# A gated mix of linear attention and a Mish MLP on one core: features sent through DRAM, and the first block's numerator as one group

## The chip, the cores and the metric

The kernel runs on one core of a Trainium2 chip, in one launch. The metric is device time in microseconds (us), the median of three runs; lower is better.

## What is computed

The input x has 2048 rows (S) of 512 features (D). A gate per row mixes two branches. Cut to what matters:

```python
g = sigmoid((x * gate_w).sum(-1, keepdims=True))
q, k, v = x @ wqkv                        # H = 32 heads of Dh = 16
pq, pk = q @ w_phi[h], k @ w_phi[h]       # per head
phi(p) = concat(softmax(p), softmax(-p))  # over the 16 features of a head, 32 in all
kv  = phi(pk)^T v ;  z = sum over rows of phi(pk)
num = phi(pq) kv ;   den = phi(pq) z + 1e-6
a   = (num / den) @ wo
b   = mish(x @ w1 + b1) @ w2              # 512 -> 1376 -> 512
out = g * a + (1 - g) * b
```

## The kernel before

Every large product is made of three float32r products on TensorE: high part times high part, high times low, low times high. So each operand has a high copy (made by ScalarE) and a low remainder (made by VectorE or GpSimd).

A first half (eight chunks of 256 rows) projects k, v and q, takes the features of k, sums kv and z, and stores the projected q of each tile of 128 rows in DRAM (`pqd`). The second half, which the change touches, runs over four blocks of 512 rows (b = 0 to 3). A block has two kinds of work:

- **The MLP.** For each of eleven slices i of the hidden features: `up` (12 matmuls, w1 times x), `mi` (Mish, ScalarE), `hi` (high copy, ScalarE), `lo` (low remainder, GpSimd, line L503), and `dn` (12 matmuls, times w2, into four PSUM banks that stay open for the whole block). The last slice's `dn` is called `df0` to `df3`, one for each tile of 128 rows.
- **The attention of four tiles t of 128 rows.** `lq` loads the projected q from `pqd`. `mx mn d0 d1` (VectorE) subtract the maximum and the minimum, `E` (ScalarE) takes the exponential, `S rS` the sums and their reciprocals, `T D m de rd sc` the denominator, `es` scales the features by it, `tr` transposes them in 32 by 32 blocks in place. `mv` moves the features of two tiles (h = 0 or 1) into the layout `eT` that TensorE needs. `nu` (32 small matmuls for each h) makes the numerator in two PSUM banks, `oh` (ScalarE) and `ol` (VectorE, L611) copy it as high and low parts, `wo` (12 matmuls a tile) multiplies by the output weights, `ag` (ScalarE) scales by the gate, `fi` (VectorE, and a store) adds the MLP part.

`XH` and `XL` make the next block's x copies, after `LX` has loaded it; `ge gg` are the gate; `WH WL` split the output weights once, in block 0; `@z` makes the sums z.

The order is written out by hand, as a string of step names for each block (`BLOCK0`, `BLOCK1`, and `BLOCK` for blocks 2 and 3). `run` calls the steps in that order; a `+` means that the step belongs to the next block. `keep_in_program_order` pins every instruction, so each engine, and SyncE's DMA queue too, executes its own instructions in the order of the string, and an instruction that waits holds up all that stand behind it on its engine. What makes an instruction wait is its operands, and its buffers: a tile of a pool comes from a ring of a few slots by tag, and a step that takes a slot waits until all readers of the slot's last tile are done. Four rings matter here:

- PSUM: `a` (three banks: `up`, `nu`, `wo`), `kv` (one bank: `nu`, `wo`), `dn` (four).
- `oh`: two slots of 128x1024. A block's four `ohl` tiles (two for each h) take turns in them.
- `E`: two slots, each the features of a pair of tiles; `eT`: two slots.
- `pq`: three slots, for the loads `lq` and the gate row.

The move of the features before:

```python
for q in range(4):
    for k in range(4):
        o = 64 * (k % 2) + 32 * (k // 2)
        pin(Sy.dma_start(eTs[h][o : o + 32, :, q, :], Ep[key, h][32 * q : 32 * q + 32, :, k * 256 : (k + 1) * 256]))
```

Of the kernel before, what the change touches and what calls it, by code (L numbers as in the profile page):

```python
# [8 lines left out]
F32 = mybir.dt.float32  # L9
# [5 lines left out]
P = 128  # L15
S = 2048
D = 512
# [41 lines left out]


BLOCK0 = """
    up0 mi0 hi0 lo0 gr lq3 ldo0 ldo1 S1 rS1 mx2 mn2 d02 d12 up1 @z mi1 hi1 lo1 T0 D0 m0 de0 rd0 sc0 es0 tr0 up2 mi2 hi2 lo2 dn0
    T1 D1 m1 de1 rd1 sc1 es1 tr1 mv0 lq0+ lq1+ mx3 mn3 d03 d13 up3 mi3 hi3 lo3 WH0 dn1
    up4 mi4 hi4 lo4 WH1 WL0 dn2 E2 S2 T2 rS2 D2 m2 de2 rd2 sc2 es2 tr2 up5 mi5 hi5 lo5 WL1 dn3 E3 ge gg up6 mi6 hi6 lo6 dn4
    up7 mi7 hi7 lo7 dn5 nu0 oh0 S3 T3 rS3 ol0 D3 m3 de3 rd3 sc3 es3 tr3 mv1 up8 mi8 hi8 lo8 dn6
    mx0+ mn0+ d00+ d10+ mx1+ mn1+ d01+ d11+ lq2+ lq3+ wo0 ag0 wo1 ag1 E0+ E1+ S0+ T0+ rS0+ D0+ m0+ de0+ rd0+ sc0+ es0+ tr0+
    up9 mi9 hi9 lo9 dn7 up10 mi10 hi10 lo10 dn8 S1+ nu1 oh1 ol1 T1+ rS1+ D1+ LX0 LX1 m1+ de1+ rd1+ sc1+ es1+ tr1+ mv0+
    XH0+ XL0+ XH1+ XL1+ dn9 wo2 ag2 wo3 ag3 df0 fi0 df1 fi1 df2 fi2 df3 fi3
"""
BLOCK1 = """  # L70
    up0 mi0 hi0 lo0 gr mx2 mn2 d02 d12 mx3 mn3 d03 d13 up1 mi1 hi1 lo1 E2 E3 S2 T2 rS2 D2 m2 de2 rd2 sc2 es2 tr2
# [17 lines left out]
def tile_gated_mix(ctx: ExitStack, tc: tile.TileContext, xT, wv, wkT, wqT, bd, w1a, w1b, b1, w2a, w2b, wo, out):  # L89
# [6 lines left out]
    pin = tc.keep_in_program_order  # L96
    V, G_, A_, Sy = nc.vector, nc.gpsimd, nc.scalar, nc.sync

    def mm(*a, **k):
        return pin(nc.tensor.matmul(*a, **k))  # L100

    def T(shape, dt, tag, bufs, name):
        nm[0] += 1
        return sp.tile(shape, dt, name=f"{name}_{nm[0]}", tag=tag, bufs=bufs)

    def k8(name, tag, dt=F32R):
        return T([P, 2048], dt, tag, 2 if tag in ("eT", "E") else 1, name)

    def k4(name, tag, dt=F32):
        return T([P, 1024], dt, tag, {"tx": 2, "oh": 2, "z": 1}[tag], name)  # L110

    def k2(name, tag, dt=F32):
        return T([P, 512], dt, tag, {"pq": 3, "io": 4, "hl": 8}[tag], name)

    def psum(name, tag, bufs={"a": 3, "dn": 4, "kv": 1}):
        nm[0] += 1
        return pp.tile([P, 512], F32, name=f"{name}_{nm[0]}", tag=tag, bufs=bufs[tag])

    def act(out_, in_, fn=AF.Copy, **k):
        return pin(A_.activation(out_, in_, fn, **k))  # L120
# [4 lines left out]
    def hv(ap):  # L125
        return ap.rearrange("p (h f) -> p h f", f=DH)

    def f32(ap):
        return ap.bitcast(F32)
# [69 lines left out]
    def at(key, name, fn):  # L199
        steps.setdefault((key, name), []).append(fn)  # L200
# [10 lines left out]
    xs, Es, vs, psA, Ep = {}, {}, {}, {}, {}  # L211
# [38 lines left out]
    def feat_ops(key, t, src, d):  # L250

        n = str(t)

        def red(name, op):
            d[name] = T([P, H], F32, name, 2, name)
            pin(V.tensor_reduce(d[name], hv(src()), axis=AX.X, op=op))  # L256

        def dd(a):
            if "E" not in d:
                pair = key, t // 2  # L260
                if key == ("A", NCH - 1):
                    d["E"] = k4("E", "oh")
                else:
                    if pair not in Ep:
                        Ep[pair] = k8("E", "E", F32)[:, :].rearrange("p (t x) -> p t x", t=2)
                    d["E"] = Ep[pair][:, t % 2, :]
            E = hv(d["E"][:, a * 512 : (a + 1) * 512])
            if a == 0:
                pin(V.tensor_sub(E, hv(src()), d["mx"][:, :, None].to_broadcast([P, H, DH])))
            else:  # L270
                pin(V.tensor_sub(E, d["mn"][:, :, None].to_broadcast([P, H, DH]), hv(src())))  # L271

        def ss():
            d["S"] = T([P, 2 * H], F32, "Sm", 2, "Sm")
            pin(V.tensor_reduce(d["S"], hv(d["E"][:, :]), axis=AX.X, op=ALU.add))  # L275

        at(key, "mx" + n, lambda: red("mx", ALU.max))
        at(key, "mn" + n, lambda: red("mn", ALU.min))
        at(key, "d0" + n, lambda: dd(0))
        at(key, "d1" + n, lambda: dd(1))  # L280
        at(key, "E" + n, lambda: act(d["E"], d["E"], AF.Exp))
        at(key, "S" + n, ss)
        at(key, "rS" + n, lambda: pin(V.reciprocal(d["S"], d["S"])))

    def scale_by(d, eng):
        pin(eng.tensor_mul(hv(d["E"][:, :]), hv(d["E"][:, :]), d["S"][:, :, None].to_broadcast([P, 2 * H, DH])))  # L286
# [189 lines left out]

    def b_ops(b):
        key = ("B", b)
        U, dn, eTs, num, ohl, io = {}, {}, {}, {}, {}, {}

        def up(i):
            f = ORDER[i]
# [63 lines left out]
        for t in range(4):  # L546
            d = {}

            def lq(t=t, d=d):
                i = 4 * b + t  # L550
                d["p"] = k2("pq", "pq")
                pin(Sy.dma_start(d["p"], pqd[i * P : (i + 1) * P, :]))

            def tm(d=d):
                d["T"] = k4("T", "tx")
                pin(V.tensor_mul(d["T"], d["E"], B["zb"]))  # L556

            def dsum(d=d):
                d["D"] = T([P, 2 * H], F32, "Dn", 2, "Dn")
                pin(V.tensor_reduce(d["D"], hv(d["T"][:, :]), axis=AX.X, op=ALU.add))  # L560

            def de(d=d):
                d["d"] = T([P, H], F32, "den", 2, "den")
                pin(V.scalar_tensor_tensor(d["d"], d["D"][:, :H], 1e-6, d["D"][:, H:], op0=ALU.add, op1=ALU.add))  # L564

            def sc(d=d):
                sv = d["S"][:, :].rearrange("p (a h) -> p a h", a=2)
                pin(V.tensor_mul(sv, sv, d["d"][:, None, :].to_broadcast([P, 2, H])))

            def tr(d=d):  # L570
                pin(V.transpose(d["E"][:, :], d["E"][:, :]))

            at(key, f"lq{t}", lq)
            feat_ops(key, t, lambda d=d: d["p"][:, :], d)
            at(key, f"T{t}", tm)
            at(key, f"D{t}", dsum)
            at(key, f"m{t}", lambda d=d: pin(V.tensor_mul(d["D"], d["D"], d["S"])))
            at(key, f"de{t}", de)
            at(key, f"rd{t}", lambda d=d: pin(V.reciprocal(d["d"], d["d"])))
            at(key, f"sc{t}", sc)  # L580
            at(key, f"es{t}", lambda d=d: scale_by(d, V))
            at(key, f"tr{t}", tr)


        for h in range(2):
            def mv(h=h):
                eTs[h] = k8("eT", "eT", F32)[:, :].rearrange("p (t q x) -> p t q x", t=2, q=4)
                for q in range(4):
                    for k in range(4):
                        o = 64 * (k % 2) + 32 * (k // 2)  # L590
                        pin(Sy.dma_start(eTs[h][o : o + 32, :, q, :], Ep[key, h][32 * q : 32 * q + 32, :, k * 256 : (k + 1) * 256]))  # L591

            def nu(h=h):
                ev = eTs[h][:, :, :, :].rearrange("p t q (b c) -> p b (t q) c", c=32)
                po = [psum("num", tag) for tag in (("a", "a") if b and h else ("kv", "a"))]
                for bh in range(2):
                    for c in range(4):
                        u = 4 * bh + c
                        for r in range(2):
                            mm(po[r][32 * c : 32 * c + 32, bh * SC : (bh + 1) * SC], kvb[64 * r : 64 * r + 64, u, :], ev[64 * r : 64 * r + 64, u, :, :], start=True, stop=True, skip_group_check=True)  # L600
                for r in range(2):
                    num[h, r] = po[r]

            def oh(h=h):
                for gp in range(2):
                    ohl[h, gp] = k4("ohl", "oh", F32R)
                    act(ohl[h, gp][:, :512], num[h, gp])

            def ol(h=h):
                for gp in range(2):  # L610
                    pin(V.tensor_sub(ohl[h, gp][:, 512:], num[h, gp], f32(ohl[h, gp][:, :512])))  # L611

            at(key, f"mv{h}", mv)
            at(key, f"nu{h}", nu)
            at(key, f"oh{h}", oh)
            at(key, f"ol{h}", ol)
# [59 lines left out]
    for b in range(NB):  # L676
        b_ops(b)
# [47 lines left out]
    for j in range(2):  # L725
        h, l = [w[:, 2 * j : 2 * j + 2, :].rearrange("p k f -> p (k f)") for w in (wvh, wvl)]
# [94 lines left out]
```

## Time and profile before

| | |
|---|---|
| median of 3 runs | 451.55 us (450.78 to 451.81) |
| the profiled execution | 449.86 us, of which the span is 448.1 us |
| TensorE (PE) busy | 442.7 us, 99% of the span |
| VectorE (DVE) busy | 312.6 us, 70% |
| ScalarE (ACT) busy | 194.0 us, 43% |
| GpSimd (POOL) busy | 162.2 us, 36% |
| mean granted TensorE clock | 0.999 |
| DMA traffic | 40.20 MB in 27177 packets, mean 90 GB/s |

A busy share says how long an engine had an instruction in hand; matmuls are pipelined, so a busy TensorE can still have small holes. Times in the traces are microseconds from the start of the span. PEld is TensorE's weight load, SPq is SyncE's DMA queue. In a group of rows, "x12" is the number of instructions; in brackets stand the idle time before and who ended it.

### The profile page before, as it was taken

To read this page: it belongs to the slowest core of one execution; us is meant where nothing else is said; L and a number is where in the kernel's file an instruction comes from. 1 tells how busy PE (TensorE), PEld (TensorE's weight loads), DVE (VectorE), ACT (ScalarE), POOL (GpSimd) and SP (SyncE) were. 2 spreads that over 40 slices of the span, in tenths; PEclk is the share of its full clock that TensorE was granted. 3 is DMA by queue.
4 is the path that set the end of the run, shared out by engine and by line. 5 is a ranking of instruction groups with operands and counts; after the bars stand their busy time and mean duration, and the time that the engine had idled before them with its cause. 6 is when DMAs were issued, how large, how long until landed. Compare 5 with 4: busy or idle time off the path is not lost.

```text
span 448.1 us, 7219 instructions
## 1 busy us (share of the span) xinstructions
PE 442.7 (99%) x2878; PEld 363.5 (81%) x2878; DVE 312.6 (70%) x412; ACT 194.0 (43%) x267; POOL 162.2 (36%) x101
## 2 busy tenths in 40 slices
PE   8999999999999999999999999999999999999997
PEld 7888888888888888778788878888878888887885
DVE  3797658559399999999989998369769329701103
ACT  3644433444325457527165352644262653242330
POOL 3448686677862253511132220214220222221121
PEclk9999999999999999999999999999999999999999
DMA  7721522514511122313433141321231302030002
GB/s 270 272 95 47 191 80 84 191 32 155 190 49 47 48 65 66 93 49 90 147 99 136 40 151 53 88 95 47 66 123 48 94 2 94 17 78 1 0 1 94
DMA packets 27177, 40.20 MB, mean 90 GB/s; under 512 B 6916, under 2 KB 15620, under 8 KB 27144
## 3 DMA queue, kind: packets, MB, share of 16 engines
q1 hardware_dynamic: 26824, 39.35, 28.0%
q8 instruction: 22, 0.36, 0.3%
q10 hardware_dynamic: 288, 0.39, 0.3%
q14 instruction: 11, 0.09, 0.1%
q0 software_dynamic: 32, 0.01, 0.0%
HBM read 22.82 MB, written 8.40 MB: 70 GB/s over the span
## 4 chain that ended last, share of the span: by engine, by line
PE 87%; DVE 9%; SPq 2%; issue 1%; DMA 0%; ACT 0%; DVEq 0%
PE proj L100 27%; PE down L100 23%; PE up L100 22%; PE wo L100 10%; PE num L100 2%; SPq L591 2%; PE kvp L100 1%; PE warm L100 1%; DVE xbl L409 1%; DVE Sm L275 1%; PE fuse L100 1%; DVE E L286 1%; DVE T L556 1%; DVE E L271 1%; DVE den L564 1%
## 5 line engine op out<-in xcount | busy, mean ns | idle before, releaser
L503 POOL TENSOR_TENSOR l<-act,h 128x512 fp32r<-128x512 f32 x44 | 62.6, 1425 | 222.1 <-ACT h L120 203.1
L120 ACT ACTIVATE act<-up,b1s 128x512 f32<-128x512 f32 x44 | 30.2, 687 | 87.6 <-PE up L100 86.7
L324 POOL TENSOR_TENSOR zacc<-zacc,E 128x1024 f32<-128x1024 f32 x16 | 39.7, 2482 | 42.7 <-DVE E L286 41.4
L120 ACT ACTIVATE E<-E 128x1024 f32<-128x1024 f32 x32 | 33.5, 1059 | 41.0 <-DVE E L271 40.9
L286 DVE TENSOR_TENSOR E<-E,Sm 128x1024 f32<-128x1024 f32 x32 | 45.6, 1426 | 1.1
L100 PE MATMUL wo<-woh,ohl 128*128 128x512 f32 x128 | 41.2, 389 | 0.0
L275 DVE TENSOR_REDUCE Sm<-E 128x64 f32<-128x1024 f32 x32 | 38.5, 1204 | 1.5 <-ACT E L120 1.5
L100 PE MATMUL down<-w2ah,h 128*128 128x512 f32 x96 | 37.6, 392 | 0.0
L100 PE MATMUL down<-w2al,h 128*128 128x512 f32 x96 | 37.4, 390 | 0.0
L100 PE MATMUL down<-w2ah,l 128*128 128x512 f32 x96 | 37.4, 389 | 0.0
L256 DVE TENSOR_REDUCE mx<-proj 128x32 f32<-128x512 f32 x16 | 11.0, 689 | 30.7 <-PE proj L100 30.7
L100 PE MATMUL down<-w2bh,h 128*128 128x512 f32 x78 | 30.6, 392 | 0.0
L409 DVE TENSOR_TENSOR xbl<-xraw,xbh 128x1024 fp32r<-128x1024 f32 x8 | 12.0, 1528 | 26.5 <-ACT xbh L120 26.5
L100 PE MATMUL down<-w2bl,h 128*128 128x512 f32 x78 | 30.4, 390 | 0.0
L100 PE MATMUL down<-w2bh,l 128*128 128x512 f32 x78 | 30.3, 389 | 0.0
L120 ACT ACTIVATE h<-act 128x512 fp32r<-128x512 f32 x44 | 27.8, 632 | 1.4
L100 PEld LDWEIGHTS wo<-woh,ohl 128*128 128x128 f32 x128 | 24.0, 188 | 5.0
L120 ACT ACTIVATE io<-wo,g_sb 128x512 f32<-128x512 f32 x16 | 10.9, 689 | 35.3 <-PE wo L100 35.3
L120 ACT ACT_TABLE_LOAD x19 | 24.4, 1283 | 3.8 <-PE up L100 3.5
L100 PE MATMUL up<-xbh,w1ah 128*128 128x512 f32 x96 | 25.8, 390 | 0.0
L100 PE MATMUL up<-xbl,w1ah 128*128 128x512 f32 x96 | 25.7, 389 | 0.0
L100 PE MATMUL up<-xbh,w1al 128*128 128x512 f32 x96 | 25.7, 389 | 0.0
(120 smaller groups left out, 971.5 us busy)
## 6 DMA issues: line engine op xcount, KB each, us to landing
eT<-E SPq DMA_DIRECT2D x128, 64.0 KB, 2.0
xraw<-in_xT_dram SPq DMA_DIRECT2D x15, 512.0 KB, 4.6
pqd<-qs SPq DMA_DIRECT2D x16, 256.0 KB, 3.1
pq<-pqd SPq DMA_DIRECT2D x16, 256.0 KB, 2.9
out_dram<-io SPq DMA_DIRECT2D x15, 256.0 KB, 2.1
raw<-in_w1a_dram SPq DMA_DIRECT2D x3, 512.0 KB, 4.4
raw<-in_w2a_dram SPq DMA_DIRECT2D x3, 512.0 KB, 4.2
wT<-in_wkT_dram SPq DMA_DIRECT2D x4, 256.0 KB, 4.5
```

The lines of the kernel that those rows point to most:

```text
L100: return pin(nc.tensor.matmul(*a, **k))
L120: return pin(A_.activation(out_, in_, fn, **k))
L256: pin(V.tensor_reduce(d[name], hv(src()), axis=AX.X, op=op))
L271: pin(V.tensor_sub(E, d["mn"][:, :, None].to_broadcast([P, H, DH]), hv(src())))
L275: pin(V.tensor_reduce(d["S"], hv(d["E"][:, :]), axis=AX.X, op=ALU.add))
L286: pin(eng.tensor_mul(hv(d["E"][:, :]), hv(d["E"][:, :]), d["S"][:, :, None].to_broadcast([P, 2 * H, DH])))
L324: at(key, f"z{t}", lambda d=d: pin(G_.tensor_add(zacc, zacc, d["E"])))
L409: pin(V.tensor_sub(xb[b][1][:, :, sl], kt(raw[h], SC), f32(xb[b][0][:, :, sl])))
L503: pin(G_.tensor_sub(U[i]["l"], U[i]["a"], f32(U[i]["h"])))
L556: pin(V.tensor_mul(d["T"], d["E"], B["zb"]))
L564: pin(V.scalar_tensor_tensor(d["d"], d["D"][:, :H], 1e-6, d["D"][:, H:], op0=ALU.add, op1=ALU.add))
L591: pin(Sy.dma_start(eTs[h][o : o + 32, :, q, :], Ep[key, h][32 * q : 32 * q + 32, :, k * 256 : (k + 1) * 256]))
```

## The change

Two things change.

The features go through DRAM. After `tr`, each tile's features (128x1024) are stored in a DRAM tile `ed`; `mv` then reads each tile's `ed` back with four loads (32 partitions x 4 x 256 elements each) in place of sixteen moves within SBUF for a pair. So a pair has two stores of 512 KB and eight loads of 128 KB, in all four blocks, and the store stands in SyncE's queue at the place of `tr`.

The order of block 0 changes. `nu0` and `nu1` stand together behind `dn9`, the tenth of the block's MLP tiles, and `df0` to `df3` follow them; all of `wo0` to `wo3` stand at the end of the block, with `fi` between them. `d02 d12` move behind the second tile's `tr`. In PSUM, the block's `nu` takes `kv` and `a` for h = 0 and `a` and `a` for h = 1, as the other blocks do already.

```diff
 BLOCK0 = """
-    up0 mi0 hi0 lo0 gr lq3 ldo0 ldo1 S1 rS1 mx2 mn2 d02 d12 up1 @z mi1 hi1 lo1 T0 D0 m0 de0 rd0 sc0 es0 tr0 up2 mi2 hi2 lo2 dn0
-    T1 D1 m1 de1 rd1 sc1 es1 tr1 mv0 lq0+ lq1+ mx3 mn3 d03 d13 up3 mi3 hi3 lo3 WH0 dn1
+    up0 mi0 hi0 lo0 gr lq3 ldo0 ldo1 S1 rS1 mx2 mn2 up1 @z mi1 hi1 lo1 T0 D0 m0 de0 rd0 sc0 es0 tr0 up2 mi2 hi2 lo2 dn0
+    T1 D1 m1 de1 rd1 sc1 es1 tr1 mv0 lq0+ lq1+ d02 d12 mx3 mn3 d03 d13 up3 mi3 hi3 lo3 WH0 dn1
     up4 mi4 hi4 lo4 WH1 WL0 dn2 E2 S2 T2 rS2 D2 m2 de2 rd2 sc2 es2 tr2 up5 mi5 hi5 lo5 WL1 dn3 E3 ge gg up6 mi6 hi6 lo6 dn4
-    up7 mi7 hi7 lo7 dn5 nu0 oh0 S3 T3 rS3 ol0 D3 m3 de3 rd3 sc3 es3 tr3 mv1 up8 mi8 hi8 lo8 dn6
-    mx0+ mn0+ d00+ d10+ mx1+ mn1+ d01+ d11+ lq2+ lq3+ wo0 ag0 wo1 ag1 E0+ E1+ S0+ T0+ rS0+ D0+ m0+ de0+ rd0+ sc0+ es0+ tr0+
-    up9 mi9 hi9 lo9 dn7 up10 mi10 hi10 lo10 dn8 S1+ nu1 oh1 ol1 T1+ rS1+ D1+ LX0 LX1 m1+ de1+ rd1+ sc1+ es1+ tr1+ mv0+
-    XH0+ XL0+ XH1+ XL1+ dn9 wo2 ag2 wo3 ag3 df0 fi0 df1 fi1 df2 fi2 df3 fi3
+    up7 mi7 hi7 lo7 dn5 S3 T3 rS3 D3 m3 de3 rd3 sc3 es3 tr3 mv1 up8 mi8 hi8 lo8 dn6
+    mx0+ mn0+ d00+ d10+ mx1+ mn1+ d01+ d11+ lq2+ lq3+ E0+ E1+ S0+ T0+ rS0+ D0+ m0+ de0+ rd0+ sc0+ es0+ tr0+
+    up9 mi9 hi9 lo9 dn7 up10 mi10 hi10 lo10 dn8 dn9 S1+ nu0 nu1 oh0 ol0 T1+ df0 df1 oh1 rS1+ D1+ LX0 LX1 ol1 df2 df3
+    wo0 ag0 m1+ de1+ rd1+ sc1+ es1+ fi0 XH0+ XL0+ wo1 ag1 fi1 wo2 ag2 XH1+ XL1+ fi2 tr1+ mv0+ wo3 ag3 fi3
 """
...
-            def tr(d=d):
+            def tr(t=t, d=d):
                 pin(V.transpose(d["E"][:, :], d["E"][:, :]))
+                ed[t] = tc.dram_tile([P, 2 * D], F32, name=f"ed{4 * b + t}")
+                pin(Sy.dma_start(ed[t], d["E"]))
...
                 eTs[h] = k8("eT", "eT", F32)[:, :].rearrange("p (t q x) -> p t q x", t=2, q=4)
-                for q in range(4):
+                for t in range(2):
+                    src = ed[2 * h + t].rearrange("(q p) x -> p q x", q=4)
                     for k in range(4):
                         o = 64 * (k % 2) + 32 * (k // 2)
-                        pin(Sy.dma_start(eTs[h][o : o + 32, :, q, :], Ep[key, h][32 * q : 32 * q + 32, :, k * 256 : (k + 1) * 256]))
+                        pin(Sy.dma_start(eTs[h][o : o + 32, t, :, :], src[:, :, k * 256 : (k + 1) * 256]))
...
-                po = [psum("num", tag) for tag in (("a", "a") if b and h else ("kv", "a"))]
+                po = [psum("num", tag) for tag in (("kv", "a"), ("a", "a"))[h]]
```

The strings of the other blocks are unchanged; in block 1 the steps around the third and fourth tile read `S3 T3 rS3 D3 m3 de3 rd3 sc3 es3 tr3 lq0+ lq1+ mv1 up3 ... mx0+ mn0+ d00+ d10+`.

More of the change, by code (lines that the diff above doesn't have):

```diff
@@ L478, in b_ops @@
         key = ("B", b)
-        U, dn, eTs, num, ohl, io = {}, {}, {}, {}, {}, {}
+        U, dn, eTs, num, ohl, io, ed = {}, {}, {}, {}, {}, {}, {}
         def up(i):
```

## The prediction

> **What bounds the kernel now.** I read the profile's page first, then what TensorE waited for, then the chain of waits.
>
> ```profile
> PE 442.7 (99%) x2878; PEld 363.5 (81%) x2878; DVE 312.6 (70%) x412; ACT 194.0 (43%) x267; POOL 162.2 (36%) x101
> PE 87%; DVE 9%; SPq 2%; issue 1%; DMA 0%; ACT 0%; DVEq 0%
> PE num L100 <- DMA eT<-E: 0.8, 1, 0.8
> ```
>
> TensorE is busy for 99% and in the whole of the second half waits once: at block 0's first `nu`, for the moved features. The chain shows what that costs:
>
> ```profile
> 190.44 1.60 PE num L100 x32
> 192.04 2.94 PE up L100 x12
> 214.02 1.02 PE num L100 x32
> 215.05 2.94 PE down L100 x12
> 226.15 8.16 PE up L100 x36
> 261.51 2.72 PE down L100 x12
> 264.23 1.89 PE num L100 x64
> 266.12 2.99 PE down L100 x12
> 269.10 5.44 PE wo L100 x24
> ```
>
> Twelve matmuls take 2.72 us everywhere, so TensorE's own work can't be shortened by an order; an order only removes or makes holes. Block 0's first `nu`: 0.83 waited, 1.60, and 0.22 more in the tile behind it (2.94 for 2.72), 2.65 in all. The second: 1.02 + 0.22, with rounding 1.25. Block 1 has both as one group: 1.89 + 0.27 = 2.16. The change makes block 0 like block 1, so it can gain 2.65 + 1.25 - 2.16 = **1.74 us**, and nothing else in the chain is there to gain.
>
> **What it adds: three new holes in TensorE's work.** In each an in-order engine, off the path until now, gets to set it.
>
> *First, `dn9` waits for `h9` (block 0).* Today `wo0 wo1 wo2 wo3` and the two `nu` stand among the last MLP tiles and give ScalarE time. Moved to the end, they uncover this:
>
> ```profile
> 189.22 0.39 PE L100 MATMUL down<-w2ah,l 128*128 128x512 f32 x1
> 205.97 0.69 DVE L271 TENSOR_TENSOR E<-mn,pq 128x512 f32<-128x512 f32 x1
> 206.69 1.06 ACT L120 ACTIVATE E<-E 128x1024 f32<-128x1024 f32 x1 [0.45 <-DVE E L271]
> 209.79 0.63 ACT L120 ACTIVATE h<-act 128x512 fp32r<-128x512 f32 x1
> 210.55 1.31 POOL L503 TENSOR_TENSOR l<-act,h 128x512 fp32r<-128x512 f32 x1 [12.69 <-ACT h L120]
> ```
>
> `dn5` issues its last matmul at 189.22, so the next tile can start at 189.45 (pitch 0.23, 2.72 over 12). Now `up8 dn6 up9 dn7 up10 dn8` follow without a gap, six tiles of 2.72, and `dn9` wants to start at 205.77. Its `h9` stands on ScalarE behind `E1+`, which waits for VectorE's `d11+`. From the end of `d11+` (206.66) to the end of `h9` (210.42) it is 3.76, to the end of `l9` on POOL (211.86) 5.2. So I need the new end of `d11+`. VectorE is never idle on the way there:
>
> ```profile
> 159.90 0.68 DVE L269 TENSOR_TENSOR E<-pq,mx 128x512 f32<-128x512 f32 x1
> 173.81 2.29 DVE L564 SCALAR_TENSOR_TENSOR den<-Dn 128x32 f32<-128x32 f32 x1
> 180.35 2.70 DVE L269 TENSOR_TENSOR E<-pq,mx 128x512 f32<-128x512 f32 x1
> 192.71 0.13 DVE L537 TENSOR_SCALAR ge_sb<-ge_sb 128x4 f32<-128x4 f32 x1
> 193.16 1.21 DVE L275 TENSOR_REDUCE Sm<-E 128x64 f32<-128x1024 f32 x1
> 195.42 0.54 DVE L283 RECIPROCAL Sm<-Sm 128x64 f32<-128x64 f32 x1
> 195.88 1.22 DVE L611 TENSOR_TENSOR ohl<-num,ohl 128x512 fp32r<-128x512 f32 x2
> 201.83 0.65 DVE L256 TENSOR_REDUCE mx<-pq 128x32 f32<-128x512 f32 x1
> 180.12 2.39 POOL L433 TENSOR_TENSOR wol<-raw,woh 128x1024 fp32r<-128x1024 f32 x1
> ```
>
> A tile of features (`S` to `tr`) takes 201.83 - 193.16 - 1.2 (the `ol` pair in it) = 7.5, without `S` (1.1) and `rS` (195.42 to 195.88) 5.9; eight operations `mx0+` to `d11+` take 206.66 - 201.83 = 4.8. From 159.90 on the new order has two tiles of 5.9, `d02 d12` 1.2 (two of the eight), `mx3` to `d13` 2.4, two tiles of 7.5, the gate 0.4 (192.71 to 193.16) and the 4.8: 35.6 us. Today's stretch has the `ol` pair too, 36.8, and takes 46.8: 10.0 are lost, as the rows at 173.81 and 180.35 show (the latter took 2.70 where the first row took 0.68, and ended with POOL's 2.39). An operation with two SBUF operands waits for POOL's subtraction, and the other way round; sums and transposes don't. POOL's ten subtractions stay, but meet other operations. Walking the new order with that rule I lose 1.3 at `de0`, 0.8 at `T1`, 2.3 at `d12` and 1.9 at `m2` (behind the two `wol`), 0.8 at `sc2`, 0.4 at `m3` and 0.3 in small ones, an estimate of 7.8: `d11+` ends at 159.9 + 35.6 + 7.8 = 203.3. Then `h9` is there at 207.1 (a wait of 1.3), and the third matmul, due 0.45 later, waits about 0.9 more for `l9` at 208.5: **2.2 us**. With 6 to 10 us lost, 0.5 to 4.5.
>
> *Second, `wo2` waits for `oh1` (block 0).* The tag `oh` has two slots and a block four `ohl` tiles. `oh1` now stands ahead of `wo0` on ScalarE, and can write only when `wo1`, the slots' last reader, is done with them; `ag0`, `XH0+` and all else on ScalarE queue behind it. `wo2` needs the bank `kv`, which `ag0` empties. So behind `wo1`'s last matmul stand in series the second half of `oh1` and `ag0`:
>
> ```profile
> 215.14 1.09 ACT L120 ACTIVATE ohl<-num 128x512 fp32r<-128x512 f32 x2 [2.38 <-PE num L100]
> 200.46 0.69 ACT L120 ACTIVATE io<-wo,g_sb 128x512 f32<-128x512 f32 x1 [4.03 <-PE wo L100]
> ```
>
> 0.55 + 0.69 and two hand-overs of about 0.1: **1.45 us** (1.25 to 2.0). The x copies of block 1 are no third wait here: `XH1+` follows `ag2`, and `wo3` (2.72) covers both.
>
> *Third, block 1's `mx0+` waits for its loads.* SyncE's queue holds `lq0+ lq1+` behind `tr3`. Until now `tr` issued no DMA, so the two loads left early; now the store of `tr3` stands ahead of them and waits for VectorE.
>
> ```profile
> 238.73 0.94 SPq L552 DMA_DIRECT2D pq<-pqd  x2
> 252.44 10.18 SPq L591 DMA_DIRECT2D eT<-E  x16
> 252.30 0.65 DVE L256 TENSOR_REDUCE mx<-pq 128x32 f32<-128x512 f32 x1
> 266.92 1.25 DVE L611 TENSOR_TENSOR ohl<-num,ohl 128x512 fp32r<-128x512 f32 x2
> DMA to landing us min/median/max: 2.6/2.9/5.7
> xraw<-in_xT_dram SPq DMA_DIRECT2D x15, 512.0 KB, 4.6
> ```
>
> The loads leave at 238.73 (0.47 each), and `mx0+` starts at 252.30 right behind `tr3`. In the changed kernel (times relative to the block's start) the store leaves at 252.44 and the first load 0.5 later. The line of landing times is for `pq`: 255.5 by its shortest, 258.6 by its longest. I take 256.4, its median 2.9 and 0.6 for the store's 512 KB ahead of it on the same queue, so VectorE is 4.1 us late (3.2 to 6.3). `E1+`, the gate and `tr0+` move with it, and so does `ol0`, whose first half empties the bank that `wo0` needs: 267.55 today, 1.55 ahead of `wo0` at 269.10. TensorE loses 4.1 - 1.5 = **2.6 us**; from both ends, with up to 0.6 regained where a meeting with POOL falls away, 1.1 to 4.8. Part of it shows earlier, as `nu1` waits for `mi7`.
>
> Block 2 has the same order, but a cover:
>
> ```profile
> 321.40 0.68 DVE L271 TENSOR_TENSOR E<-mn,pq 128x512 f32<-128x512 f32 x1
> 326.26 2.01 ACT L120 ACTIVATE E<-E 128x1024 f32<-128x1024 f32 x2
> ```
>
> There `d11+` ends at 322.08, and ScalarE comes to `E1+` only at 327.3: 5.2 us to spare against 4.1. Block 3 loads nothing. Both cost nothing; at the far end of 6.3 block 2 would cost 1.1.
>
> **What I cost at nothing.** `d02 d12` behind `tr1`: `E2` then waits for `d12` until 177.4 in my walk, and `h5` follows 3.76 later by the same chain as above, 181.2; `dn5` starts at 189.45 - 2.72 = 186.7, 5.5 to spare. `LX0 LX1` behind the store of `tr0+` in SyncE's queue: `LX1` waits for `D1+` anyway, about 217.5, lands 4.6 later at 222.1, and `XH1+` comes behind `wo2`, about 225.7. The other banks for `nu`: its last `a` bank waits for `mi10`, one ScalarE step (0.7) behind `h9`, at 207.8; `nu1` comes at 211.6 (below).
>
> **The route through DRAM itself**: nothing, as long as it lands in time.
>
> ```profile
> 179.31 10.20 SPq L591 DMA_DIRECT2D eT<-E  x16
> eT<-E SPq DMA_DIRECT2D x128, 64.0 KB, 2.0
> raw<-in_wo_dram SPq DMA_DIRECT2D x8, 128.0 KB, 3.1
> ```
>
> Today a pair lands 10.2 + 2.0 behind its `tr`. Now: the store 4.6, four loads at 10.2 / 16 = 0.64 each 2.6, landing 3.1: 10.3 (the other four go out while the store lands). In block 0 `tr3` ends at 203.3 - 4.8 = 198.5, so it lands at 208.8, and `nu1` comes at 205.77 + 2.2 + 2.72 + 0.95 = 211.6. The Trainium skill ("DMA: Bandwidth & Descriptors", "Anatomy of one DMA") puts a DMA at 2.0 us plus its bytes over 436 GB/s, measured on another issue path, and says that completion takes longest where HBM is written: by it the store is 3.2 and the sum the same. No run here shows a 512 KB store yet.
>
> **The sum.** -1.74 + 2.2 + 1.45 + 2.6 = +4.5 us. Against the profiled execution: 449.86 + 4.5 = 454.4. That execution lies 1.69 under the median of the runs; on the median, 451.55 + 4.5 = **456.0 us**. All low ends give +1.1, all high ends +9.6.
>
> **The rivals.**
> - *Not slower: VectorE escapes POOL.* If the new order meets none of POOL's subtractions in block 0, `d11+` ends at 195.5 and `dn9` doesn't wait; if block 1's `tr3` comes 2 us early likewise, the late loads cost 0.6 at most. Then -1.74 + 1.45 + 0 to 0.6: 451.3 to 451.9, no change. It decides where under 2 us are lost in block 0. For it: the losses are chance meetings. Against: ten subtractions remain and VectorE is full. Chance 0.06; a gain over 0.2% needs `oh1`'s wait gone too, which the slots forbid.
> - *Block 1's late loads are covered.* If they land sooner or the chain behind them has more room than the rows show, 2.6 drops out: 453.4. Chance 0.12.
> - *The DRAM trip is late.* If the store takes over 7.4 us (2.8 us to spare above), `nu1` waits, and in block 0 again as long as that excess, some 2 us: 458. Against: nothing else of weight is on the queue then. Chance 0.05.
> - *The clock falls.*
>
> ```profile
> 186.00:196.00 10.00, 9.17 (x66) 6.60 (x66) 9.72 (x15) 4.65 (x9) 2.53 (x2) 1.00 0.36 99
> ```
>
> In this window, with the hole of 0.83 in it, the clock granted is 1.00. At the high end of the first term `dn9` waits 3.5 in one piece, four times as long as any hole here. If the tile behind it then ran at half the clock, it would take 5.44 for 2.72: with the hole, 456.0 + 2.3 + 2.7 = 461. The Trainium skill ("TensorE: Matmul & The Clock Gate", "Part 1") has the clock halved after an idle window of about 3.4 us. No run here shows it. Chance 0.04.
>
> **How the numbers follow.** The forecast has 0.70; 0.03 is for what I haven't seen. About 0.2% (0.9 us) is what a measurement of this kernel can tell from no change. Range: down to 453.0 (block 1 covered, or two low ends), up to 459.0 (the high ends of two terms, or the late trip); outside lie "not slower", the clock, and the corners of the terms. Of the 0.06 I count 0.05 as same and 0.01 as faster, the unseen 0.03 as faster, and 0.01 of the covered case as same: faster 0.04, same 0.06, slower 0.90.
>
> **What would show it.** One `num` group of 64 in block 0, with no wait for a DMA. TensorE's waits: `down` for ACT `h` and POOL `l` (about 2), `wo` for ACT `io` (about 1.4), and in block 1 `num` and `wo` for ACT and DVE (about 2.6); VectorE waiting for `pq` in blocks 1 and 2, some 4 us each. In block 0 `d11+` ends near 203. I am wrong if `dn9` starts without a wait, or if `pq` lands ahead of `tr3`.

## The result, and the profile after

The changed kernel takes **457.69 us** (median of 5 runs, 456.93 to 459.22); the kernel before, run beside it, takes 450.93 (5 runs). The ratio is 1.0153, 95% interval 1.0130 to 1.0175: 6.8 us slower, where 4.5 were forecast on the median, and inside the range. Its profiled execution took 459.22 us with a span of 457.5, 9.4 more than the span before.

What TensorE waited for, after (total, times, longest, in us):

```profile
PE wo L100 <- DVE ohl L614: 2.1, 1, 2.1
PE down L100 <- ACT h L120: 1.3, 1, 1.3
PE wo L100 <- ACT io L120: 1.3, 1, 1.3
...
PE fuse L100 <- DMA wT<-in_wkT_dram: 0.9, 1, 0.9
PE down L100 <- POOL l L503: 0.7, 1, 0.7
```

The wait for the moved features is gone, and three holes have come: `dn9` for `h9` and `l9`, `wo2` for `ag0`, and block 1's `wo0` for `ol0`. The wait of `fuse` lies at the start, far ahead of the change, and differs from execution to execution: `dn5` ends 0.73 us later than before for that reason alone (first row below against 189.22).

The timeline of the three places, after (start, duration, engine, line, what; idle time in brackets). Line numbers behind the new store are two or three higher than before:

```profile
189.95 0.39 PE L100 MATMUL down<-w2ah,l 128*128 128x512 f32 x1
203.49 0.69 DVE L271 TENSOR_TENSOR E<-mn,pq 128x512 f32<-128x512 f32 x1
206.27 0.39 PE L100 MATMUL down<-w2bh,l 128*128 128x512 f32 x1
207.30 0.63 ACT L120 ACTIVATE h<-act 128x512 fp32r<-128x512 f32 x1
207.98 0.50 PE L100 MATMUL down<-w2bh,h 128*128 128x512 f32 x1 [1.32 <-ACT h L120]
208.06 2.54 POOL L503 TENSOR_TENSOR l<-act,h 128x512 fp32r<-128x512 f32 x2 [12.13 <-ACT h L120]
209.42 0.68 PE L100 MATMUL down<-w2bh,l 128*128 128x512 f32 x1 [0.71 <-POOL l L503]
209.90 0.63 PE L100 MATMUL down<-w2bh,h 128*128 128x512 f32 x1
212.46 0.63 PE L100 MATMUL down<-w2bh,h 128*128 128x512 f32 x1
213.49 1.96 PE L100 MATMUL num<-eT,kvb 64*32 64x256 f32 x64
223.87 0.60 ACT L120 ACTIVATE ohl<-num 128x512 fp32r<-128x512 f32 x1 [0.76 <-PE wo L100]
224.37 0.68 ACT L120 ACTIVATE io<-wo,g_sb 128x512 f32<-128x512 f32 x1
225.10 0.50 PE L100 MATMUL wo<-woh,ohl 128*128 128x512 f32 x1 [1.26 <-ACT io L120]
230.72 1.07 PE L100 MATMUL up<-xbh,w1ah 128*128 128x512 f32 x4
257.77 1.19 SPq L552 DMA_DIRECT2D pq<-pqd  x2
261.05 0.69 DVE L256 TENSOR_REDUCE mx<-pq 128x32 f32<-128x512 f32 x1 [3.68 <-DMA pq<-pqd]
268.89 2.60 PE L100 MATMUL num<-eT,kvb 64*32 64x256 f32 x64
276.54 0.50 PE L100 MATMUL wo<-woh,ohl 128*128 128x512 f32 x1 [2.07 <-DVE ohl L614]
```

Between 209.90 and 212.46 six matmuls go by: a pitch of 0.43 us where the forecast's is 0.23. The chain shows the same, and once more in block 1:

```profile
209.42 4.14 PE down L100 x10
...
218.40 5.45 PE wo L100 x24
276.54 7.35 PE wo L100 x24
```

The same 24 `wo` matmuls take 5.45 us in block 0 and 7.35 in block 1. The clock says why. The windows below lie on the grid that the clock's own changes give: each slow stretch is 3.41 us long, and from the end of the first to the start of the second it is 64.86 us, 19 times 3.41. Columns: length, PE busy (instructions), granted clock, DMA share, GB/s:

```profile
206.17:209.58 3.41, 1.38 (x6) 1.00 0.42 146
209.58:212.99 3.41, 3.41 (x9) 0.50 0.03 5
...
223.23:226.65 3.42, 2.15 (x10) 1.00 0.01 2
...
274.43:277.85 3.42, 1.35 (x7) 1.00 0.35 134
277.85:281.26 3.41, 3.41 (x10) 0.50 0.53 173
```

The window that holds both waits of `dn9` is idle for 2.03 of its 3.41 us, the one with block 1's hole for 2.07, and the window after each runs at half the clock. The one with `wo2`'s hole is idle for 1.26 and no slow one follows. A slow window costs 3.41 / 2 = 1.7 us, 0.0037 of the mean clock. The granted clocks of the five runs were 0.993, 0.993, 0.996, 0.996 and 1.000: two, two, one, one and no such windows. The median run is the one with none: its span of 454.8 us is the shortest of the five, but 2.9 us of its time lie outside the span, against 1.7 to 2.0 in the others. So the median comes out where the mean does (457.96 against 451.18 before, also 6.8 more) in part by chance.

The 9.4 us of the profiled pair then come out: 0.73 at the start; block 0 from `dn5` to block 1's first `up` 4.73 - 0.73 = 4.0 (230.72 above against the row of before below); in block 1 up to `wo0` 276.54 - 269.10 - 4.73 = 2.7; and 7.35 - 5.44 = 1.9 in the slow `wo`, of which some 0.2 is there at full clock too, as behind `wo2`'s hole. The row of before:

```profile
225.99 1.07 PE L100 MATMUL up<-xbh,w1ah 128*128 128x512 f32 x4
```

### The profile page after: what moved, and what is told of

Same layout as the page of the kernel before. It is cut to its first block, busy times and chain, and to the rows that moved or that the text cites. A ratio compares the mean times of both kernels' runs of the same rounds, so it can differ in the third digit from the quotient of the medians.

```text
span 457.5 us, 7152 instructions
## 1 busy us (share of the span) xinstructions
PE 446.4 (98%) x2878; PEld 365.1 (80%) x2878; DVE 312.6 (68%) x412; ACT 194.0 (42%) x267; POOL 160.6 (35%) x101
## 4 chain that ended last, share of the span: by engine, by line
PE 69%; DVE 23%; DMA 4%; issue 2%; ACT 1%; SPq 0%; POOL 0%; DVEq 0%; POOLq 0%
PE proj L100 25%; PE down L100 17%; PE up L100 15%; PE wo L100 9%; DVE E L286 2%; DVE Sm L275 2%; DVE T L556 2%; DVE E L571 2%; DMA wT<-in_wqT_dram 2%; DVE E L269 2%; DVE Dn L560 2%; DVE E L271 2%; DVE xbl L409 1%; DVE Dn L579 1%; DVE mn L256 1%
## 5 line engine op out<-in xcount | busy, mean ns | idle before, releaser
L503 POOL TENSOR_TENSOR l<-act,h 128x512 fp32r<-128x512 f32 x44 | 61.1, 1390 | 232.2 <-ACT h L120 210.7
L100 PE MATMUL wo<-woh,ohl 128*128 128x512 f32 x128 | 42.7, 402 | 3.3 <-DVE ohl L614 2.1
```

What stands on the lines that cost most here:

```text
L503: pin(G_.tensor_sub(U[i]["l"], U[i]["a"], f32(U[i]["h"])))
```

## The experiments

Three readings were set against each other: the **holes alone**, at the forecast's prices; **holes and clock**, where a hole can be followed by slow matmuls; and **the route**, that DRAM traffic itself costs the time. All medians:

| kernel | us | before beside it | ratio (95%) | granted clock of its runs |
|---|---|---|---|---|
| changed kernel | 457.69 | 450.93 | 1.0153 (1.0130 to 1.0175) | two at 0.993, two at 0.996, 1.000 |
| order alone | 453.92 | 451.19 | 1.0065 (1.0049 to 1.0081) | one of six at 0.995, the others 0.999 or 1.000 |
| route alone | 454.91 | 451.19 | 1.0085 (1.0059 to 1.0111) | three of six at 0.996 |
| route, early loads | 450.45 | 451.19 | 0.9984 (0.9971 to 0.9998) | all 0.999 or 1.000 |
| changed, `E0+ E1+` later | 456.39 | 451.19 | 1.0117 (1.0097 to 1.0137) | five of six at 0.996 |
| changed, `oh1` covered | 455.39 | 450.74 | 1.0095 (1.0077 to 1.0113) | 0.992, three at 0.996, two at 1.000 |
| changed, early loads | 453.24 | 450.59 | 1.0056 (1.0034 to 1.0079) | one of five at 0.996 |
| no holes | 449.24 | 450.74 | 0.9962 (0.9949 to 0.9975) | all 0.999 or 1.000 |
| no holes, old moves | 450.37 | 450.59 | 0.9992 (0.9976 to 1.0008) | all 0.999 or 1.000 |

**The order alone.** The changed kernel with the old `tr` and `mv`:

```diff
-ed[t] = tc.dram_tile(...); pin(Sy.dma_start(ed[t], d["E"]))
-pin(Sy.dma_start(eTs[h][o : o + 32, t, :, :], src[:, :, k * 256 : (k + 1) * 256]))
+pin(Sy.dma_start(eTs[h][o : o + 32, :, q, :], Ep[key, h][32 * q : 32 * q + 32, :, k * 256 : (k + 1) * 256]))
```

> The new order of block 0 and the new banks, with the old moves between SBUF tiles in place of the store and the loads. Holes alone (the forecast's terms): -1.7 for the merged num, +2.2 for dn9's wait, +1.4 for wo2's wait, nothing in block 1: 1.9 us over the kernel before. Holes and clock: the same, and where dn9's two waits fall into one stretch of some 3.4 us the following matmuls run at a pitch of 0.43 us, 1.6 to 2.1 more: 3.5 to 4.0 us over before in such a run. The route costs by itself (rival): the order alone then gives no more than 1 us over before.

Measured: 2.7 us over before (2.2 to 3.7 by the interval), more than the 1.9 of the holes alone. Its trace has the two waits of `dn9` to the hundredth, but on another phase of the grid:

```profile
208.38 0.50 PE L100 MATMUL down<-w2bh,h 128*128 128x512 f32 x1 [1.32 <-ACT h L120]
209.82 0.50 PE L100 MATMUL down<-w2bh,l 128*128 128x512 f32 x1 [0.71 <-POOL l L503]
```

```profile
205.92:209.33 3.41, 1.87 (x8) 1.00 0.38 97
209.33:212.74 3.41, 2.92 (x26) 1.00 0.62 168
```

A window's edge cuts the pair into 1.54 and 0.49 us of idle time, and the clock stays at 1.00. The same holes, with and without the slow tile: the clock's part is chance of phase, not of the kernel. The chain then shows what `dn9`'s holes cost at full clock. The ten matmuls behind the second wait:

```profile
209.82 2.60 PE down L100 x10
```

They take 2.60 where the changed kernel's took 4.14, so the slow window there cost 1.5. `dn9` was due at 206.90 (0.23 behind the last matmul of `dn8`, at 206.67) and starts at 208.38, 1.5 late; its third matmul, due 0.45 later, starts at 209.82, another 1.0 late; and some 0.2 go behind the holes. That is 2.7, not the forecast's 2.2: the waits that the profile lists (1.32 and 0.71) count only from the modelled end of the matmul before. With it the order alone costs -1.7 + 2.7 + 1.4 = 2.4, and one slow window in six runs 0.3: the measured 2.7.

**The route alone**, with the old order of block 0 and the old banks, and **the route with early loads**:

```diff
 BLOCK1: ... mx3 mn3 d03 d13
+lq0+ lq1+
 up1 ... es3 tr3
-lq0+ lq1+
 mv1 ...
 BLOCK (blocks 2, 3): up0 mi0 hi0 lo0 gr
+lq0+ lq1+
 S2 T2 ... es3 tr3
-lq0+ lq1+
 mv1 ...
```

> The store and the loads through DRAM, with the old order of block 0 and the old banks. Holes alone: block 1's mx0+ late by 3.7, TensorE loses 2.7 there; block 0's first num no longer waits for its moves (0.8 less at most): 1.9 to 2.7 us over before. Holes and clock: 1.9 more in a run where the 2.1 us before wo0 are followed by slow matmuls: 3.8 to 4.6. The route costs by itself: over 5 us.

> The route alone again, with lq0+ and lq1+ of blocks 1 and 2 put ahead of the stores in SyncE's queue. Holes alone, and holes and clock: no hole is left in block 1, the granted clock is 1.00 behind it, and the time is that of before, or up to 0.8 us less (block 0's first num without its wait). The route costs by itself: stays 2 us or more over before.

Measured: 3.7 us over before (2.7 to 5.0), and 0.7 under it (0.1 to 1.3). Moving two load instructions in a queue takes away all that the route costs, so the traffic itself costs nothing; what costs is the store that stands ahead of the loads. Nor did the first `num`'s 0.83 all come back. What TensorE waits for in the second kernel:

```profile
PE wo L100 <- DVE ohl L614: 0.9, 2, 0.6
```

These are two waits of block 0, of 0.30 and 0.55, that the kernel before doesn't have: where the features come earlier, VectorE's `ol0` and `ol1` are late.

**`dn9`'s hole taken out**:

```diff
-lq2+ lq3+ E0+ E1+ S0+ T0+ rS0+ D0+ m0+ de0+ rd0+ sc0+ es0+ tr0+ up9 mi9 hi9 lo9 dn7 up10
+lq2+ lq3+ up9 mi9 hi9 lo9 dn7 E0+ E1+ S0+ T0+ rS0+ D0+ m0+ de0+ rd0+ sc0+ es0+ tr0+ up10
```

> The changed kernel with E0+ E1+ and the steps behind them moved behind mi9 hi9 lo9, so that h9 no longer waits for VectorE's d11+. Holes alone: dn9 doesn't wait, 2.2 us under the changed kernel, 455.5. Holes and clock: 2.2 and the slow tile of 2.1 go, up to 4.3 us under the changed kernel in its slowest runs: 453.4 to 455.5, with a pitch of 0.23 us in dn9. If the clock fell for another reason than the hole, dn9 still runs at 0.43.

`dn9` doesn't wait and isn't slow, but the kernel gains only 1.3 us on the changed one's median. A new wait took the rest:

```profile
215.07 0.50 PE L100 MATMUL wo<-woh,ohl 128*128 128x512 f32 x1 [0.86 <-DVE ohl L614]
```

TensorE now comes earlier to `wo0`, and VectorE isn't ready with `ol0`, which stands behind `tr0+` and `S1+`. Of `dn9`'s 2.7 the wait and the restart behind it take back 1.1, which leaves 1.6; the clock would add up to 0.6 to that (five slow windows in six runs, against six in five). The medians show less than either, 1.3, and the expected 453.4 to 455.5 was missed; the runs don't show why beyond this wait.

**`wo2`'s hole taken out**: `oh1` and `ol1` behind `ag0` and close behind `wo1`, and half of `dn10` as cover.

```diff
-df0 df1 oh1 rS1+ D1+ LX0 LX1 ol1 df2 df3 wo0 ag0 m1+ de1+ rd1+ sc1+ es1+ fi0 XH0+ XL0+ wo1 ag1 fi1 wo2
+df0 df1 rS1+ D1+ LX0 LX1 wo0 ag0 m1+ de1+ rd1+ sc1+ wo1 oh1 ol1 es1+ ag1 XH0+ XL0+ XH1+ XL1+ df2 df3 fi0 fi1 wo2
```

> The changed kernel with oh1 and ol1 behind ag0 on ScalarE and with df2 df3 between wo1 and wo2 as cover. Holes alone: wo2's wait of 1.4 goes, dn9's and block 1's stay: 1.4 under the changed kernel, 456.2, in a run of equal granted clock. Holes and clock: the same; the clock's share of some 2 us for each slow window still comes and goes with dn9's and block 1's holes. If wo2's wait has another cause than the oh slots, it stays at 1.3.

The wait for `io` is gone, the other two stand unchanged (1.3 and 0.7; 2.1). The median is 2.3 us under the changed kernel: 1.4 for the hole, and some 0.6 for the clock, again with five slow windows in six runs. So it was `oh1`'s place ahead of `ag0`, where it waits for its slots, that cost the time.

**Block 1's hole taken out**: the changed kernel with the early loads above.

> The changed kernel with lq0+ and lq1+ of blocks 1 and 2 ahead of the stores, and nothing else. Holes alone: block 1's 2.7 us go, dn9's and wo2's stay: 455.0 from the changed kernel's 457.7. Holes and clock: with them goes the slow window behind that hole, which came in some two of three runs and costs 1.7: 453.9, that is 2.7 to 3.2 over before; the granted clock falls only where dn9's two waits lie in one window of the grid. The route costs by itself: 455 or more with no wait in block 1.

2.65 us over before, 4.45 under the changed kernel: the 2.7 of the hole, and 1.7 for one slow window a run less (one in five runs, against six). In its profiled run `dn9`'s two waits lie in one window of the grid again, with less idle time than any other that was followed by a slow one:

```profile
205.95:209.36 3.41, 1.49 (x5) 1.00 0.29 106
209.37:212.78 3.41, 3.41 (x16) 0.50 0.02 5
```

**No holes**: all three edits, with `ol0` ahead of `tr0+ S1+` and `T1+ D1+` drawn forward, so that VectorE is in time:

```diff
-es0+ tr0+ up10 mi10 hi10 lo10 dn8 dn9 S1+ nu0 nu1 oh0 ol0 T1+ df0 df1 oh1 rS1+ D1+ LX0 LX1 ol1 df2 df3 wo0 ...
+es0+ up10 mi10 hi10 lo10 dn8 dn9 nu0 nu1 oh0 ol0 T1+ D1+ LX0 LX1 tr0+ S1+ rS1+ df0 df1 wo0 ag0
+m1+ de1+ rd1+ sc1+ wo1 oh1 ol1 es1+ ag1 XH0+ XL0+ XH1+ XL1+ df2 df3 fi0 fi1 wo2 ag2 fi2 tr1+ mv0+ wo3 ag3 fi3
```

> All three holes taken out of the changed kernel: E0+ E1+ behind hi9, the features of the next block spread around the merged num so that ol0 and ol1 come in time, oh1 behind ag0 with df2 df3 as cover, lq0+ lq1+ of blocks 1 and 2 ahead of the stores. Holes alone, and holes and clock: no wait of TensorE in blocks 0 and 1 and a granted clock of 1.00, so the merged num's 1.7 us is what is left: 449.3 with before at 451.0. A new wait of up to 1 us may come for ol0 or for block 1's x copy: then 450.3. The DRAM route costs by itself: 451 or more without any wait of TensorE that shows.

449.24 us, 1.5 under before on the medians (1.1 to 2.3 by the interval) and 8.4 under the changed kernel's median. This version beats both. The chain of waits is TensorE alone through block 0's end; the two `wo` groups take 0.2 to 0.3 more than 5.44:

```profile
210.25 1.89 PE num L100 x64
212.14 1.60 PE down L100 x6
213.74 5.63 PE wo L100 x24
219.37 1.36 PE down L100 x6
220.73 5.74 PE wo L100 x24
```

**No holes, with the old moves** between SBUF tiles:

> The kernel without holes (order of block 0 as in that run, early loads), with the old moves between SBUF tiles in place of the store and the loads. If the route through DRAM is worth only its earlier landing: the moves leave behind tr3, take 10.2 and land 2.0 later, some 2.0 us behind the merged num's place, so num waits about 2 us for eT: 451.2, and in some runs 1.7 more where that hole lies in one window of the grid. If the route is worth nothing: no wait, 449.2.

Between the two: 450.37, 1.1 over the version with the route, no difference from before. The merged `num` waits for the last move. Its first 32 matmuls start at 209.29; the chain from there on, the last move's landing first:

```profile
209.14 1.99 DMA eT<-E
...
211.17 0.62 PE num L100 x2
211.79 0.23 issue
212.02 1.09 PE num L100 x30
213.11 1.59 PE down L100 x6
```

From the first `num` at 209.29 to the first `down` behind it at 213.04 it is 3.75 us, where the version with the route takes 1.89: 1.9 are lost, as expected, though the waits that the profile lists there are only 0.78 and 0.23. Some 0.5 come back, since both `wo` groups take their 5.44 here, not 5.63 and 5.74. So the route is worth its earlier landing, 1.9 us at `num` and 1.1 in all by the medians, and the order without it gains nothing.

**Holes of chosen length.** To the kernel before, waits were added that TensorE can't avoid, in blocks 1 to 3:

```diff
+t = k2("gap", "io", F32R)            # behind up_i: k copies on ScalarE, the first from up_i's bank
+act(t[:, :n], U[i]["ps"][:, :n]); act(t[:, :n], f32(t[:, :n])); ...
+ps = psum("gap", "kv"); mm(ps[:, :P], t[:, :P], t[:, :P], start=True, stop=True)
```

> The kernel before with nine waits of TensorE put in, each behind one up tile: two to five copies on ScalarE, then one small matmul that reads the last copy. From the copies' 0.55 to 0.63 us they should last about 1.5, 1.9, 2.2 (block 1), 2.5, 1.9, 2.2 (block 2), 2.8, 1.5, 3.4 us (block 3), 20 us in sum. Skill's rule, taken as a hole of 3.4 us or more: none but perhaps the last is followed by slow matmuls, 471 us in all. Fixed windows of 3.4 us, slow when idle for more than some 1.3 to 2.0 us of one: the longer holes mostly, the short ones hardly ever; the slow stretches last 3.4 us each, begin at the same phase of a 3.41 us grid, and cost 1.7 us each: four to seven of them, 478 to 483 us. A threshold on the length of a hole alone: the same holes in all runs, whatever their place on the grid.

484.49 us, above the 478 to 483 expected: the nine waits came to 23.2 us, not 20; one was 5.8 long, since its slot waited for an output store. Five windows ran slow, each behind one that was idle for 2.01 us or more. A wait of 2.46, cut by an edge, had none behind it. The largest idle time in a window without a slow one behind it was 1.82, at the end:

```profile
477.20:480.61 3.41, 1.59 (x13) 1.00 0.62 230
480.61:484.02 3.41, 0.00 (x0) 1.00 0.00 1
```

> The kernel before with eight waits of equal make-up (three copies on ScalarE, then the small matmul), 2.0 us each: 16 to 17 us, 468 us at full clock. Fixed windows of 3.41 us, slow behind any that was idle for 1.9 us or more: of the eight equal holes those that lie within one window are followed by 3.41 us at half the clock, those that a window's edge cuts are not; by the lengths, one in three to one in two, so 2 to 5 of them at 1.7 us: 471 to 476. A threshold on the hole's length: all eight or none, 481 or 468.

474.92 us. The waits in the profile (in total, times, longest):

```profile
PE gap L100 <- ACT gap L120: 16.1, 8, 2.0
```

Two of the eight equal waits lie whole in a window, and a slow one follows; six are cut by an edge, and none does. One of each kind:

```profile
244.92:248.34 3.42, 1.41 (x8) 1.00 0.00 0
248.34:251.75 3.41, 3.41 (x9) 0.50 0.00 0
258.58:261.99 3.41, 2.44 (x11) 1.00 0.39 101
261.99:265.40 3.41, 2.37 (x11) 1.00 0.43 109
```

A threshold on the length of a hole is excluded: equal holes did both.

## Why the prediction was right, and where it fell short

The direction, the three holes, their places and their releasers came as forecast. Term by term, in the profiled pair, with the order alone to split `dn9`'s holes from the clock:

| term | forecast | measured |
|---|---|---|
| two `num` groups merged | -1.74 | -1.7: from `num` at 213.49 to `wo0` at 218.40 it is 4.91, of which 2.72 is `dn10`'s own; 2.2 left, where before lost 3.9 |
| `dn9` waits for `h9`, `l9` | 2.2 (1.3 + 0.9) | 2.7: due at 206.50, starts at 207.98, 1.5; the third matmul 1.0 late again (209.42); 0.2 behind the holes |
| `wo2` behind `oh1` and `ag0` | 1.45 | 1.4: `oh1`'s second half waits for `wo1` until 223.87, `ag0` follows at 224.37; TensorE is idle for 1.26, and slower by 0.2 behind it |
| block 1's late loads | 2.6 | 2.7: 2.07 at `wo0`, and 0.6 inside `num` (2.60 for 1.96), whose last bank `mi7` empties only at 270.34 |
| sum | 4.5 | 5.1 |
| slow windows | 0 (a rival, 0.04) | 3.4 in this run: 1.5 in `dn9` (4.14 for 2.60), 1.9 in `wo` (7.35 for 5.44) |

- **VectorE's walk** through block 0 forecast the end of `d11+` at 203.3. It came at 203.49 + 0.69 - 0.73 = 203.45 on before's time. The rule read off before's rows, that operations with two SBUF operands and GpSimd's subtractions hold each other up, carried that step, and not by luck of the sum: the losses lie where the walk put them, or one operation beside it (0.9 at `T1` for 0.8, 2.2 at `d02` for 2.3 at `d12`, 1.8 at `m2` for 1.9, 1.0 each at `m0` and `es2` for 1.3 at `de0` and 0.8 at `sc2`, 0.8 at `m3` for 0.4).
- **The two `oh` slots**: right, and shown by undoing the order around them.
- **SyncE's queue**: VectorE waited 3.68 for `pq` where 4.1 was forecast, and again in block 2 (3.7), where it cost nothing, as forecast. Two loads moved ahead of the stores took it away.
- **The route costs nothing in itself**: right. The DMA rows after (KB, median us to landing):

```profile
ed<-E SPq DMA_DIRECT2D x16, 512.0 KB, 2.9
eT<-ed SPq DMA_DIRECT2D x64, 128.0 KB, 3.4
```

  I had the store at 4.6, from the slowest near row; it took 2.9. The estimate of 3.2 from the Trainium skill ("DMA: Bandwidth & Descriptors", "Anatomy of one DMA") was the nearer. Neither decided anything.
- **The step that was mis-sized** is the rival "the clock falls". It was put at 0.04, with the condition that `dn9` wait 3.5 us in one piece, and priced at 2.7 behind that. The runs show another condition: 1.92 us or more of idle time, in one piece or two, inside one window of a fixed grid of 3.41 us; up to 1.82 did nothing. Both larger holes could meet it, each by the luck of its phase. The row that I gave against it, a clock of 1.00 with a hole of 0.83, lies far below the threshold and said nothing of holes of 2 us. Six slow windows in five runs make 6 x 1.7 / 5 = 2.0 us on the mean, and 5.1 + 2.0 = 7.1 stands against the measured 6.8. The error of 2.3 us is in the main that term; 0.5 is `dn9`'s, and what is over lies within the scatter of the start (0.73 in the profiled pair). That the time still lies inside the range is in part luck: the range's top was drawn for the high ends of the other terms, and the profiled run, at 459.22, lies above it.
- The Trainium skill ("TensorE: Matmul & The Clock Gate", "Part 1") speaks of a free-running window of 3413 ns, and the slow stretches here agree, 3.41 us on a fixed grid. It has the clock halved after an idle window of about 3.4 us; by that neither hole of the changed kernel would have slowed anything, and the measurement differs.
- **"A gain over 0.2% needs `oh1`'s wait gone too, which the slots forbid"** was too strong. The slots forbid it in the order as written; with half of `dn10` as cover, the same two slots do.

## What to carry to other kernels

Where TensorE is busy for 99%, a reordering is worth the holes it makes less the ones it removes; follow each in-order queue, the DMA queue too, to what now stands ahead of the work that a hole waits for. A store that waits for its producer, put in a queue ahead of loads that were ready, delayed them here by 3.7 us, and moving two words in the order took that away. Price a hole of about 2 us or more with the clock in it: where it fills more than some 1.9 of a 3.41 us window, the next 3.41 us cost some 1.7 more.

## What the runs showed of the hardware

- In the kept traces, from 8 us into the span on, the granted clock went to 0.50 for one window of 3.41 us behind every window in which TensorE was idle for 1.92 us or more, and behind none idle for 1.82 or less. Idle time in one window adds up over two waits (1.32 and 0.71).
- One kernel's runs differ in the number of slow windows, with the place of its holes on the grid: the changed kernel's spans run from 454.8 at a clock of 1.000 (none) to 457.5 at 0.993 (two).
- A 512 KB store of SBUF to DRAM landed in 2.9 us, and four loads of 128 KB behind it in 3.4 each, without a wait that TensorE felt.
